# An attention and MLP kernel: the first batch's pieces in another hand-written order, two units' queries transposed twice, other engines for some copies

## The chip, the cores and the metric

The kernel runs on one core of a Trainium2 chip (trn2). The metric is the device time of one execution in microseconds (us); the kernel before was executed three times without the profiler, and once more with it. Engines are named as in the profile: PE (TensorE matmuls) and PEld (its weight loads), DVE (VectorE), ACT (ScalarE), POOL (GpSimd), SP (SyncE, which here only issues transfers). Each engine works through its own queue in order and waits on semaphores for what the others produce.

## The reference

For each of 8 batches and 12 heads, attention with normalised queries and keys, over 448 tokens and 64 columns a head; then, for each token, a normalisation over the 768 joined columns and a two-layer MLP that is added to its input.

```
def rmsnorm(x, g):
    rms = np.sqrt(np.mean(x * x, axis=-1, keepdims=True) + 1e-06)
    return x / rms * g
q_n, k_n = (rmsnorm(q, g_q), rmsnorm(k, g_k))
scores = np.matmul(q_n, k_n.transpose(0, 1, 3, 2)) / np.sqrt(64)
attn = softmax(scores)                      # written out in the original
x = np.matmul(attn, v)                      # heads joined: (8, 448, 768)
xn = (x - mean(x)) / np.sqrt(var(x) + 1e-06) * g_ln
out = x + np.maximum(xn @ w_ch1, 0.0) @ w_ch2   # 768 -> 3072 -> 768
```

## The kernel before

**Units, pairs, groups.** Two heads make a pair; a batch has 6 pairs. Pairs are prepared in units: batch 0 has units 0 and 1 of one pair each (pairs 0 and 1), units 2 and 3 of two pairs each (2 and 3, 4 and 5); every later unit has two pairs. A pair's 448 tokens form 7 groups of 128 rows: six of 128 tokens of one head, and one with the last 64 tokens of both heads.

**Preparing a unit.** `pieces` gives each step a letter, which the order below uses: b begin, a and c the squares of keys and queries (`square`), d and e their sums (`total`), g, gk, gq the reciprocal roots (`root`: two short ACT instructions), i the keys times the product of the two gains (`kg`), j the keys' high part in 16 bits (`khi`), k their low part (`klo`), l the scaled queries (`qn`), m a second copy of the queries beside the first (`qdup`), z the values. Constants at the head of the file say which engine does a step for which unit: `DVE_KG`, `POOL_HI`, `POOL_DUP`, `POOL_SQUARE`, `POOL_LO`, and `ACT_Q`, `ACT_K`, `ACT_DUP` for copies that otherwise go to DVE or POOL. The keys' high and low parts stand side by side as 128 columns, so that one product with the doubled queries adds both.

**Transposes.** K*p* (`trans_k`) transposes pair p's seven key groups by small matmuls with an identity into the PSUM tile "tr" and copies them to `kU`; Q*p* (`trans_q`) does the same with the queries, for pairs of batch 0 by way of a PSUM tile "psQ" of its own, for pair 6 and later by "tr". Units listed in `TWICE` skip the copy m: `trans_q` transposes the 64 query columns twice, into partitions 0 to 63 and into 64 to 127, by two half-width matmuls a group.

**Attention.** S*p.i* (`scores`) multiplies one group's keys with all queries into one of two PSUM banks "psS", and ACT takes the exponential (line 433), which frees the bank. The seventh group of the first units takes two accumulating matmuls (lines 427, 428). V*p.i* (`values`) multiplies the exponentials with the values (lines 470, 472); after i = 6, DVE divides (lines 485 to 492). T*p* gathers statistics on DVE.

**The order.** For batch 0 the whole work is written out by hand in `ORDER`: `first_attention` goes through it and records each piece on its engine, and this is the order of every engine's queue. It holds seven pairs' scores (pair 6 is batch 1's first). H*n* stands for n matmuls of the identity with itself on a PSUM tile "psW" that nothing reads (line 544), J*n* for n such on "tr" (line 547). L*u* loads unit u by SP, W*c* loads weights by POOL's queue, A, N, X, R are the first MLP's normalisation and its transposes (line 710), U*t* the first products of the MLP (line 956). After it, `run_rest` runs batch b's MLP on PE (first lines 730 and 740, later 809 and 832) with the next batch's attention spread between its matmuls.

Of the kernel before, what the change touches and what calls it, by code (L numbers as in the profile page):

```python
# [34 lines left out]


ORDER = """
b0 H12 a0 L4 c0 i0 e0 j0 H24 b1 gq0 d0 k0 l0 a1 m0 K0 G gk0 i1 H10 L5 c1 Q0 d1 j1 H8 S0.0 b2  # L40
S0.1 H5 a2 e1 g1 S0.2 c2 S0.3 k1 l1 z0 d2 e2 m1 K1 S0.4 i2 H16 S0.5 S0.6 H12 Q1 g2 H5 J8 b3 l2
j2 k2 c3 V0.0 S1.0 z2 S1.1 S1.2 V1.0 J8 a3 m2 H4 V0.1 z3 S1.3 K2 S1.4 V0.2 Q2 V0.3 V0.4 d3 S1.5
V0.5 V0.6 S2.0 S1.6 V1.1 V1.2 S2.1 e3 W0 i3 K3 V2.0 S2.2 V2.1 S2.3 Q3 j3 T0 S2.4 k3 V1.3 g3 V1.4
S2.5 S2.6 l3 b4 V1.5 m3 c4 S3.0 S3.1 V2.2 S3.2 K4 a4 V1.6 S3.3 V2.3 S3.4 Q4 d4 V2.4 V2.5 V3.0
V3.1 V3.2 V2.6 i4 S3.5 j4 J4 S3.6 V3.3 T1 K5 e4 k4 S4.0 W1 S4.1 S4.2 Q5 z4 b5 S4.3 V3.4 V4.0
V3.5 S4.4 V4.1 V4.2 S4.5 W2 V4.3 S5.0 g4 V3.6 S4.6 S5.1 J4 V5.0 V4.4 G2 S5.2 l4 T3 K6 V4.5 V5.1
V4.6 S5.3 T4 V5.2 a5 L6 V5.3 S5.4 m4 Q6 i5 S5.5 V5.4 S5.6 V5.5 V5.6 T5 S6.0 S6.1 J4 S6.2 A V6.0
S6.3 V6.1 N0 N1 S6.4 S6.5 J4 V6.2 X0 V6.3 d5 j5 N2 S6.6 V6.4 X1 z5 Q7 c5 V6.5 R U0 e5 U1 g5 X2
V6.6 M k5 U2 K7 b6 L7 a6 L8k c6 i6 l5 m5 e6
""".split()  # L50
# [44 lines left out]
class _Fast:  # L95
# [141 lines left out]
    def pieces(self, u):  # L237
# [91 lines left out]
        def qdup():  # L329
            if u in TWICE:  # L330
                return
            out, x = c["qn"][:, :, 1], c["qn"][:, :, 0]
            if u in ACT_DUP:
                nc.scalar.copy(out=out, in_=x)
            else:
                (nc.gpsimd if u in POOL_DUP else nc.vector).tensor_copy(out=out, in_=x)
# [50 lines left out]
    def trans_q(self, p):  # L387
# [6 lines left out]
        for i in (6, *range(6)):  # L394
            o, g = ps[:, :, 384:S] if i == 6 else ps[:, i // 3, ts(i % 3, 128)], self.group(p, i)
            for r in (slice(0, D), slice(D, 2 * D)) if u in TWICE else (slice(0, 2 * D),):
                nc.tensor.matmul(o[r], qn[:, g, 0] if u in TWICE else qn[:, g], sh.id16,
                                 is_transpose=True, start=(i == 6), stop=(i == 5))
# [866 lines left out]
```

## Time and profile before

| What | us |
| --- | --- |
| median of 3 runs | 578.69 |
| lowest and highest | 578.44, 578.82 |
| the profiled execution | 578.23 |
| its span, first to last instruction | 576.70 |
| PE busy in the span | 563.6 (98%) |
| PEld | 416.5 (72%) |
| DVE | 385.5 (67%) |
| ACT | 363.4 (63%) |
| POOL | 210.0 (36%) |

The rows shown further on come from the profiled execution; times in them count from the start of its span. A row of the timeline has start, length, engine, line, operation, output<-inputs, how many instructions it merges, and in brackets how long the engine was idle before it and what ended that. Matmuls are pipelined, so the length of one is more than the distance to the next; the same holds, by about 0.1 us, for neighbouring ACT and DVE instructions. A row of the stretches has the length of the stretch, each engine's busy time and instructions, the TensorE clock's granted share, the DMA engines' share and GB/s.

### The profile page before, as it was taken

How to read it: one execution, taken by the hardware profiler on the slowest of the kernel's cores; microseconds unless marked ns; L12 is line 12 of the kernel's file. 1: busy time of each engine (PE TensorE's matmuls, PEld its weight loads, DVE VectorE, ACT ScalarE, POOL GpSimd, SP SyncE). 2: the span in 40 equal slices, each digit the busy share in tenths (PEclk: the TensorE clock that was granted, in tenths of full speed). 3: DMA queues.
4: the chain of work that ended last, by engine and by line, in shares of the span. 5: the costliest groups of instructions: out<-in, count | busy, mean ns of one | idle time of the engine just before them, and what ended most of it. 6: DMA issues, size and time to landing. Idle time of an engine off the chain costs nothing.

```text
span 576.7 us, 13800 instructions
## 1 busy us (share of the span) xinstructions
PE 563.6 (98%) x5510; PEld 416.5 (72%) x5510; DVE 385.5 (67%) x832; ACT 363.4 (63%) x672; POOL 210.0 (36%) x226
## 2 busy tenths in 40 slices
PE   6888999999999999999999999999999999999999
PEld 5656666687686867777677768777777777878686
DVE  6989578799757586846667586854756743664424
ACT  5998886457674779457675588647777477323130
POOL 4885855404540721554341521654242410020000
PEclk9999999999999999999999999999999999999999
DMA  8999999968573877968563787958753390030302
GB/s 215 272 237 221 212 200 165 170 180 111 124 134 84 145 151 141 127 140 116 124 91 66 183 139 143 117 139 141 129 62 65 120 112 2 1 109 1 84 2 59
DMA packets 175321, 72.59 MB, mean 126 GB/s; under 512 B 138292, under 2 KB 170212, under 8 KB 175252
## 3 DMA queue, kind: packets, MB, share of 16 engines
q1 hardware_dynamic: 134304, 52.75, 43.9%
q0 software_dynamic: 40352, 18.50, 24.1%
q8 instruction: 44, 0.72, 0.5%
q10 hardware_dynamic: 596, 0.41, 0.3%
q14 instruction: 25, 0.20, 0.1%
HBM read 52.76 MB, written 11.01 MB: 111 GB/s over the span
## 4 chain that ended last, share of the span: by engine, by line
PE 92%; DVE 3%; ACT 3%; issue 1%; DMA 0%; ACTq 0%; DVEq 0%
PE psH L809 34%; PE psP L832 30%; PE psS L417 8%; PE oA L470 5%; PE psC L740 4%; PE psH L730 4%; ACT E L433 2%; PE oB L472 2%; PE psS L423 2%; DVE ssq L269 1%; PE psW L544 1%; PE tr L380 1%; ACT qU L400 0%; PE psW L1003 0%; DMA w<-in_g_k_dram 0%
## 5 line engine op out<-in xcount | busy, mean ns | idle before, releaser
L433 ACT ACTIVATE E<-psS,rr_all 128x448 f16<-128x448 f32 x336 | 204.1, 633 | 49.1 <-PE psS L417 40.4
L809 PE MATMUL psH<-xnT,w 128*128 128x256 f16 (+1 forms) x2016 | 225.7, 261 | 0.0
L809 PEld LDWEIGHTS <-w 128*128 128x128 f16 x2016 | 172.8, 98 | 24.4 <-issue 5.0
L812 ACT ACTIVATE hS<-psH 128x512 f16<-128x512 f32 x150 | 89.7, 598 | 98.0 <-PE psH L809 93.3
L832 PEld LDWEIGHTS <-hS 128*128 128x128 f16 x1080 | 100.0, 98 | 57.4 <-issue 1.1
L832 PE MATMUL psP<-w,hS 128*128 128x384 f16 x672 | 127.0, 326 | 0.0
L417 PE MATMUL psS<-qU,kU 128*128 128x448 f16 x288 | 101.0, 352 | 4.4 <-ACT E L433 2.9
L470 PEld LDWEIGHTS <-E 128*128 128x128 f16 x1008 | 70.3, 98 | 35.6 <-issue 2.6
L283 POOL TENSOR_TENSOR k<-k,gprod 128x896 f32<-128x896 f32 x18 | 39.2, 2180 | 139.8 <-ACT khl L263 86.1
L815 DVE TENSOR_TENSOR hS<-hS 128x512 f16<-128x512 f16 (+1 forms) x119 | 58.3, 496 | 19.3 <-ACT hS L812 17.8
L832 PE MATMUL psP<-w2s,hS 128*128 128x384 f16 (+1 forms) x408 | 69.9, 322 | 0.0
L470 PE MATMUL oA<-v,E 128*128 128x65 f16 x864 | 66.8, 194 | 1.1 <-ACT E L433 0.6
L768 DVE SCALAR_TENSOR_TENSOR x<-psP,rs_all,x 128x384 f32<-128x384 f32 x60 | 36.4, 616 | 41.1 <-PE psP L832 40.5
L472 PE MATMUL oB<-v,E 128*128 128x65 f16 x288 | 52.0, 193 | 0.1
L843 POOL TENSOR_TENSOR x<-x,hS 128x384 f32<-128x384 f32 x21 | 23.4, 1126 | 75.3 <-ACT hS L911 74.6
L485 DVE RECIPROCAL rec_all<-oA 128x6 f32<-128x6 f32 x48 | 9.2, 192 | 53.0 <-PE oA L470 52.9
L220 POOL DMA_DIRECT2D v<-in_v_dram x54 | 41.5, 781 | 4.4 <-PE oB L472 3.3
L417 PEld LDWEIGHTS <-kU 128*128 128x128 f16 x288 | 28.1, 98 | 10.7 <-issue 2.0
L911 ACT ACTIVATE hS<-hS,rs_all 128x384 f32<-128x384 f32 x27 | 14.6, 604 | 33.0 <-DVE hS L815 33.0
L472 PEld LDWEIGHTS <-E 128*128 128x128 f16 x336 | 32.4, 97 | 0.3 <-DVE xl L492 0.2
L86 DVE SCALAR_TENSOR_TENSOR qn<-q,rr_all 128x256 f16<-128x256 f32 (+2 forms) x69 | 25.0, 424 | 6.8 <-ACT rr_all L273 6.7
L269 DVE TENSOR_REDUCE ssq<-khl 128x14 f32<-128x896 f32 (+1 forms) x24 | 25.5, 1061 | 3.7 <-ACT khl L263 3.6
(145 smaller groups left out, 630.5 us busy)
## 6 DMA issues: line engine op xcount, KB each, us to landing
k<-in_k_dram SPq DMA_DIRECT2D x19, 384.0 KB, 4.3
q<-in_q_dram SPq DMA_DIRECT2D x18, 384.0 KB, 4.1
out_dram<-x SPq DMA_DIRECT2D x14, 384.0 KB, 3.0
w<-in_moe_w_ch_dram POOLq DMA_DIRECT2D x3, 1536.0 KB, 14.5
w<-in_moe_w_ch_dram POOLq DMA_DIRECT2D x4, 1152.0 KB, 14.1
v<-in_v_dram POOLq DMA_DIRECT2D x54, 64.0 KB, 4.4
out_dram<-x POOLq DMA_DIRECT2D x9, 384.0 KB, 2.7
qU<-qn SPq DMA_TRANSPOSE x90, 2.9
```

Source lines behind the costliest of these rows:

```text
L220: nc.gpsimd.dma_start(out[:, :, j, 0:D], main[:, :, j])
L269: nc.vector.tensor_reduce(out=c["ssq"][:, n], in_=c["sq", n], axis=AX.X, op=ALU.add)
L283: (nc.vector if u in DVE_KG else nc.gpsimd).tensor_tensor(out=c["t"][1], in0=c["t"][1], in1=sh.gprod.unsqueeze(1).broadcast_to([128, g, D] ...
L417: nc.tensor.matmul(ps[0][:, 0:S], c["main"][:, ts(i, 128)], c["q"][:, ts(h, S)], start=True, stop=True)
L433: nc.scalar.activation(out=o, in_=x[:, 0:S], func=AFT.Exp, scale=self.units[u][3][:, g:g + 1], bias=EXP_BIAS)
L470: nc.tensor.matmul(oA[:, t, cs], E[:, ts(t, 128)], rhs, start=(i == 0 and t == 0), stop=(i == 6 and t == 2))
L472: nc.tensor.matmul(oB[:, cs], E[:, 320:448], rhs, start=(i == 0), stop=(i == 6))
L768: self.nc.vector.scalar_tensor_tensor(out=x, in0=ps, scalar=self.rs[:, b, t:t + 1], in1=x, op0=ALU.mult, op1=ALU.add)
L809: nc.tensor.matmul(ps[:, i], sh.w1[:, dc, ts(f + i, 128)], self.xnT[:, dc, 256 - N:256], start=(i == 0 and dc == 0), stop=(i == k - 1 and ...
L812: nc.scalar.activation(out=hT[:, f:f + k], in_=ps, func=AFT.Relu)
L815: nc.vector.tensor_tensor(out=out, in0=a, in1=c, op=op)
L832: nc.tensor.matmul(bank[x][:, c], a[:, f], w[:, f, c], start=(start and f == 0), stop=(stop and f == HALF - 1))
```

## The change

`ORDER` is rewritten; it holds the same 218 pieces of work. Its identity matmuls on "psW" go from 96 to 144, those on "tr" from 32 to 4. Units 0 and 2 skip the second copy of their queries: the 21 query transposes of pairs 0, 2 and 3 become 42 of half width. Together PE gets 41 matmuls more. Homes that change: unit 1's and unit 2's key multiply from POOL to DVE, unit 6's from DVE to POOL; unit 1's high part from POOL to ACT; unit 1's second query copy from DVE to ACT; pair 0's key copy out of PSUM from DVE to ACT; pair 0's and pair 2's query copy from ACT to DVE; the square of unit 6's queries from POOL to ACT. SP's queue stays as it was.

```
-DVE_KG, POOL_HI, POOL_DUP, ACT_Q = (0, 6), (1, 2, 3, 4, 5, 6, *range(8, 25)), (3, 4, 5, 6), (0, 2, 4, 5)
-ACT_K, ACT_DUP = (), ()
+DVE_KG, POOL_HI, POOL_DUP, ACT_Q = (0, 1, 2), (2, 3, 4, 5, 6, *range(8, 25)), (1, 3, 4, 5, 6), (4, 5)
+ACT_K, ACT_DUP = (0,), (0, 1, 2)
 END_WORK = 44
-TWICE = ()
-POOL_SQUARE, POOL_LO = ((2, 1), (4, 0), (6, 0), (7, 0), (7, 1)), (5, 6)
+TWICE = (0, 2)
+POOL_SQUARE, POOL_LO = ((2, 1), (4, 0), (7, 0), (7, 1)), (5, 6)

 ORDER = """
-b0 H12 a0 L4 c0 i0 e0 j0 H24 b1 gq0 d0 k0 l0 a1 m0 K0 G gk0 i1 H10 L5 c1 Q0 d1 j1 H8 S0.0 b2
-S0.1 H5 a2 e1 g1 S0.2 c2 S0.3 k1 l1 z0 d2 e2 m1 K1 S0.4 i2 H16 S0.5 S0.6 H12 Q1 g2 H5 J8 b3 l2
-j2 k2 c3 V0.0 S1.0 z2 S1.1 S1.2 V1.0 J8 a3 m2 H4 V0.1 z3 S1.3 K2 S1.4 V0.2 Q2 V0.3 V0.4 d3 S1.5
-V0.5 V0.6 S2.0 S1.6 V1.1 V1.2 S2.1 e3 W0 i3 K3 V2.0 S2.2 V2.1 S2.3 Q3 j3 T0 S2.4 k3 V1.3 g3 V1.4
...
-V3.5 S4.4 V4.1 V4.2 S4.5 W2 V4.3 S5.0 g4 V3.6 S4.6 S5.1 J4 V5.0 V4.4 G2 S5.2 l4 T3 K6 V4.5 V5.1
-V4.6 S5.3 T4 V5.2 a5 L6 V5.3 S5.4 m4 Q6 i5 S5.5 V5.4 S5.6 V5.5 V5.6 T5 S6.0 S6.1 J4 S6.2 A V6.0
-S6.3 V6.1 N0 N1 S6.4 S6.5 J4 V6.2 X0 V6.3 d5 j5 N2 S6.6 V6.4 X1 z5 Q7 c5 V6.5 R U0 e5 U1 g5 X2
-V6.6 M k5 U2 K7 b6 L7 a6 L8k c6 i6 l5 m5 e6
+b0 H26 L4 b1 a0 c0 i0 e0 j0 gq0 G a1 k0 H10 l0 d0 H9 c1 i1 gk0 L5 d1 m0 K0 H8 Q0 e1 j1 b2 k1 H13
+S0.0 a2 S0.1 H26 H10 g1 i2 c2 S0.2 S0.3 H4 l1 m1 d2 H8 z0 j2 S0.4 V0.0 H2 e2 H5 S0.5 g2 Q1 K1 b3
+z2 c3 H8 z3 V0.1 H7 V0.2 S1.0 l2 S0.6 V0.3 k2 m2 S1.1 a3 H8 d3 V0.4 S1.2 V0.5 V1.0 S1.3 V1.1 K2
+S1.4 Q2 S1.5 S1.6 V0.6 S2.0 S2.1 e3 T0 S2.2 V1.2 V2.0 g3 V2.1 S2.3 i3 j3 k3 W0 K3 S2.4 V2.2 Q3
...
+V3.6 S4.5 W2 V4.0 V4.1 V4.2 g4 V4.3 S4.6 G2 S5.0 K6 T3 V4.4 S5.1 l4 V5.0 S5.2 S5.3 V5.1 V5.2
+S5.4 m4 V4.5 L6 V4.6 S5.5 T4 S5.6 b5 V5.3 a5 Q6 V5.4 V5.5 V5.6 S6.0 i5 T5 S6.1 J4 S6.2 S6.3 S6.4
+V6.0 S6.5 A N0 N1 V6.1 X0 V6.2 S6.6 X1 N2 Q7 V6.3 U0 d5 j5 R X2 V6.4 V6.5 U1 L7 L8k c5 M K7 e5
+U2 z5 b6 V6.6 a6 k5 g5 l5 m5 c6 i6 e6
 """.split()
```

More of the change, by code (lines that the diff above doesn't have):

```diff
@@ L27 @@
 EXP_BIAS = -4.0
-DVE_KG, POOL_HI, POOL_DUP, ACT_Q = (0, 6), (1, 2, 3, 4, 5, 6, *range(8, 25)), (3, 4, 5, 6), (0, 2, 4, 5)
-ACT_K, ACT_DUP = (), ()
+DVE_KG, POOL_HI, POOL_DUP, ACT_Q = (0, 1, 2), (2, 3, 4, 5, 6, *range(8, 25)), (1, 3, 4, 5, 6), (4, 5)
+ACT_K, ACT_DUP = (0,), (0, 1, 2)
 END_WORK = 44
-TWICE = ()
-POOL_SQUARE, POOL_LO = ((2, 1), (4, 0), (6, 0), (7, 0), (7, 1)), (5, 6)
+TWICE = (0, 2)
+POOL_SQUARE, POOL_LO = ((2, 1), (4, 0), (7, 0), (7, 1)), (5, 6)
 ORDER = """
-b0 H12 a0 L4 c0 i0 e0 j0 H24 b1 gq0 d0 k0 l0 a1 m0 K0 G gk0 i1 H10 L5 c1 Q0 d1 j1 H8 S0.0 b2
-S0.1 H5 a2 e1 g1 S0.2 c2 S0.3 k1 l1 z0 d2 e2 m1 K1 S0.4 i2 H16 S0.5 S0.6 H12 Q1 g2 H5 J8 b3 l2
-j2 k2 c3 V0.0 S1.0 z2 S1.1 S1.2 V1.0 J8 a3 m2 H4 V0.1 z3 S1.3 K2 S1.4 V0.2 Q2 V0.3 V0.4 d3 S1.5
-V0.5 V0.6 S2.0 S1.6 V1.1 V1.2 S2.1 e3 W0 i3 K3 V2.0 S2.2 V2.1 S2.3 Q3 j3 T0 S2.4 k3 V1.3 g3 V1.4
-S2.5 S2.6 l3 b4 V1.5 m3 c4 S3.0 S3.1 V2.2 S3.2 K4 a4 V1.6 S3.3 V2.3 S3.4 Q4 d4 V2.4 V2.5 V3.0
-V3.1 V3.2 V2.6 i4 S3.5 j4 J4 S3.6 V3.3 T1 K5 e4 k4 S4.0 W1 S4.1 S4.2 Q5 z4 b5 S4.3 V3.4 V4.0
-V3.5 S4.4 V4.1 V4.2 S4.5 W2 V4.3 S5.0 g4 V3.6 S4.6 S5.1 J4 V5.0 V4.4 G2 S5.2 l4 T3 K6 V4.5 V5.1
-V4.6 S5.3 T4 V5.2 a5 L6 V5.3 S5.4 m4 Q6 i5 S5.5 V5.4 S5.6 V5.5 V5.6 T5 S6.0 S6.1 J4 S6.2 A V6.0
-S6.3 V6.1 N0 N1 S6.4 S6.5 J4 V6.2 X0 V6.3 d5 j5 N2 S6.6 V6.4 X1 z5 Q7 c5 V6.5 R U0 e5 U1 g5 X2
-V6.6 M k5 U2 K7 b6 L7 a6 L8k c6 i6 l5 m5 e6
+b0 H26 L4 b1 a0 c0 i0 e0 j0 gq0 G a1 k0 H10 l0 d0 H9 c1 i1 gk0 L5 d1 m0 K0 H8 Q0 e1 j1 b2 k1 H13
+S0.0 a2 S0.1 H26 H10 g1 i2 c2 S0.2 S0.3 H4 l1 m1 d2 H8 z0 j2 S0.4 V0.0 H2 e2 H5 S0.5 g2 Q1 K1 b3
+z2 c3 H8 z3 V0.1 H7 V0.2 S1.0 l2 S0.6 V0.3 k2 m2 S1.1 a3 H8 d3 V0.4 S1.2 V0.5 V1.0 S1.3 V1.1 K2
+S1.4 Q2 S1.5 S1.6 V0.6 S2.0 S2.1 e3 T0 S2.2 V1.2 V2.0 g3 V2.1 S2.3 i3 j3 k3 W0 K3 S2.4 V2.2 Q3
+S2.5 V1.3 b4 S2.6 V1.4 S3.0 a4 S3.1 V2.3 c4 V1.5 S3.2 l3 V1.6 V2.4 V2.5 d4 T1 S3.3 m3 S3.4 Q4
+V3.0 K4 i4 S3.5 j4 e4 S3.6 Q5 W1 V3.1 V2.6 V3.2 V3.3 S4.0 K5 V3.4 S4.1 V3.5 S4.2 z4 S4.3 S4.4 k4
+V3.6 S4.5 W2 V4.0 V4.1 V4.2 g4 V4.3 S4.6 G2 S5.0 K6 T3 V4.4 S5.1 l4 V5.0 S5.2 S5.3 V5.1 V5.2
+S5.4 m4 V4.5 L6 V4.6 S5.5 T4 S5.6 b5 V5.3 a5 Q6 V5.4 V5.5 V5.6 S6.0 i5 T5 S6.1 J4 S6.2 S6.3 S6.4
+V6.0 S6.5 A N0 N1 V6.1 X0 V6.2 S6.6 X1 N2 Q7 V6.3 U0 d5 j5 R X2 V6.4 V6.5 U1 L7 L8k c5 M K7 e5
+U2 z5 b6 V6.6 a6 k5 g5 l5 m5 c6 i6 e6
 """.split()
```

## The prediction

> **What bounds the kernel now.** I read the page first, then a table of stretches, then each engine's timeline from 0 to 57 us, where all of the change lies. The table gives each stretch's length and each engine's busy us, with instruction counts:
>
> ```profile
> core 0: us, PE busy (x) PEld busy (x) DVE busy (x) ACT busy (x) POOL busy (x), PEclk, DMA share, GB/s
> 0.00:12.90 12.90, 8.11 (x72) 7.22 (x73) 8.00 (x21) 5.84 (x12) 5.29 (x12) 1.00 0.83 205
> 12.90:51.20 38.30, 31.62 (x411) 21.84 (x410) 35.45 (x68) 35.52 (x67) 28.15 (x27) 1.00 1.09 250
> ...
> 56.40:576.70 520.30, 519.07 (x4948) 382.78 (x4945) 336.94 (x735) 318.34 (x586) 172.40 (x184) 1.00 0.65 114
> ```
>
> From 56.4 us on TensorE is busy 519.07 of 520.30 us, so nothing but TensorE work sets that stage, and a shift of its start passes to the end one for one. Before that, three stages: a start in which one chain runs from the first load to the first exponential; 38 us in which ScalarE holds 35.5 us of work; and a tail of transposes and first products. The 49 exponentials of the middle (42 of the first six pairs, 7 of the seventh):
>
> ```profile
> L433 ACT ACTIVATE E<-psS,rr_all 128x448 f16<-128x448 f32 x49 | 28.4, 631 | 2.3 <-PE psS L417 1.8
> L400 ACT COPY qU<-psQ 128x896 f16<-128x896 f16 x3 | 2.7, 908 | 0.0
> ```
>
> **The start, step by step.** These are the rows up to the first exponential (start, length):
>
> ```profile
> 2.73 1.46 PE L544 MATMUL psW<-id 128*128 128x128 f16 x12 [2.73 <-POOL id masks.py:199]
> 5.70 0.69 PE L281 MATMUL psG<-gprod,w 1*128 1x64 f32 x2 [1.51 <-DVE gprod L278]
> 6.32 2.74 PE L544 MATMUL psW<-id 128*128 128x128 f16 x24
> 9.09 0.85 PE L380 MATMUL tr<-id,khl 128*128 128x128 f16 x6
> 9.73 1.27 PE L544 MATMUL psW<-id 128*128 128x128 f16 x10
> 10.80 0.74 PE L397 MATMUL psQ<-id,qn 128*128 128x128 f16 x7
> 11.37 0.61 PE L544 MATMUL psW<-id 128*128 128x128 f16 x8
> 12.53 0.54 PE L417 MATMUL psS<-qU,kU 128*128 128x448 f16 x2 [0.55 <-ACT qU L400]
> ...
> 7.81 0.61 DVE L269 TENSOR_REDUCE ssq<-w2s 128x7 f32<-128x448 f32 x1
> 8.34 0.62 DVE L294 TENSOR_TENSOR khl<-w2s,khl 128x448 f16<-128x448 f32 x1
> 8.87 0.62 DVE L86 SCALAR_TENSOR_TENSOR qn<-w2s,rr_all 128x448 f16<-128x448 f32 x1
> 9.52 1.11 DVE L336 COPY qn<-qn 128x448 f16<-128x448 f16 x1
> ...
> 8.93 1.55 POOL L283 TENSOR_TENSOR w2s<-w2s,gprod 128x448 f32<-128x448 f32 x1 [4.92 <-ACT khl L263]
> ...
> 7.40 0.58 ACT L291 ACTIVATE khl<-w2s 128x448 f16<-128x448 f32 x1 [1.26 <-DVE w2s L283]
> 11.57 0.91 ACT L400 COPY qU<-psQ 128x896 f16<-128x896 f16 x1 [1.81 <-PE psQ L397]
> 12.91 1.16 ACT L433 ACTIVATE E<-psS,rr_all 128x448 f16<-128x448 f32 x2 [0.44 <-PE psS L417]
> ```
>
> Queries of unit 0 are normalised until 9.49, copied beside themselves until 10.63 (1.11 us, drawn out by the POOL multiply, which ends at 10.48), transposed from 10.80, copied out by ScalarE until 12.48, and the first exponential begins at 12.91. TensorE's clock is seen in the spacing of equal small matmuls: 24 in 2.74 us stand (2.74 - 0.31) / 23 = 106 ns apart, 10 from 9.73 still 106 ns, 8 from 11.37 (0.61 - 0.22) / 7 = 56 ns. So full speed comes at about 11.2 us, inside the seven query transposes, 5.5 us after TensorE became steadily busy at 5.70.
>
> In the changed queues the copy L336 of unit 0 is gone, and one reduction (L269, step 8.34 - 7.81 = 0.53 us) moves behind the low-part subtraction L294. That then waits only for ScalarE's cast, until 7.40 + 0.58 = 8.0, and the normalisation L86 ends near 8.0 + 0.53 + 0.62 = 9.2 instead of 9.49. TensorE: 26 fillers to about 5.5, psG, 19 fillers from 6.32 to 8.35, the key transposes from about 8.7, 8 fillers, then the queries. At the slow clock this puts the queries at 8.7 + 7 x 0.107 + 8 x 0.107 = 10.3, at the fast one at 8.7 + 15 x 0.056 = 9.5.
>
> The query transposes are now 14 of half width, which write partitions 0 to 63 and 64 to 127 in turn. No transpose like that is in the trace; the nearest rows are the leftover scores of later units, 64 weight columns each and the two halves alternating:
>
> ```profile
> L423 PEld LDWEIGHTS <-kU x80: 106/108/110, 73.9 to 482.8; 128*64 128x64 f16 x80
> ...
> 73.90 0.59 PE L423 MATMUL psS<-qU,kU 128*64 128x448 f16 x4
> ...
> 74.42 1.15 PE L730 MATMUL psH<-w2s,w 128*128 128x384 f16 x6
> ```
>
> Four of them take 0.59 us with a median length of 0.37, so the first and the last start 0.22 us apart: two pairs, each pair side by side (one after the other it would be 3 x 0.187 = 0.56). A pair of 448 columns takes 0.21 where 448 columns alone take 0.187, so 23 ns are added for each pair; and the next full-width matmul stands 0.52 - 0.21 - 0.19 = 0.12 us late. I take 0.1 us at each end of a group and 23 ns a pair: 14 cost 0.2 + 7 x 0.078 = 0.75 us fast and 0.2 + 7 x 0.13 = 1.1 us slow. Bounds: 7 x 0.056 = 0.4 us (pairs for nothing), and 14 x 0.108 = 1.5 us (each behind its own 108 ns weight load). For the 42 half-width transposes of pairs 0, 2 and 3 the upper bound is 2.2 us above my price. The lower one is 1.1 us below it.
>
> VectorE, not ScalarE, now copies these queries out (0.62 us, by the L402 row below), but two reductions and unit 1's key multiply stand before it until about 10.7. So at the fast clock the copy ends near 11.3; at the slow clock the transposes end at 11.5 and the copy at 12.1. ScalarE meanwhile copies the keys, 128x960 out of PSUM, which no row shows: 0.91 x 960 / 896 = 0.97 by the L400 row (not under the 0.62 of VectorE, not over 1.3, twice an exponential of half the size), and casts unit 1's keys (0.58, as the first cast L291 of this shape), which holds it to about 11.6. The first score and 0.4 us later the first exponential: 11.8 to 12.5 instead of 12.91. **Start: -0.4 us if the clock is released when it was, -1.1 us if before 9.5 us.**
>
> **The clock.** TensorE will be busy from 2.73 with one hole of 0.2 us (5.5 to 5.7) where it stood idle from 4.19 to 5.70. Counting 5.5 us of steady work as in the row above puts the release at 8.2; if it hangs on the moment and not on the work, at 11.2. The Trainium skill, TensorE: Matmul & The Clock Gate, Part 1, says that a busy window of about 3.4 us that runs freely releases the clock; by that rule it would come between 6.1 and 9.6, and the trace's 5.5 us neither confirms nor excludes it.
>
> **The middle.** ScalarE waits that show:
>
> ```profile
> 17.60 0.91 DVE L336 COPY qn<-qn 128x448 f16<-128x448 f16 x1
> 18.56 0.56 PE L397 MATMUL psQ<-id,qn 128*128 128x128 f16 x7 [0.47 <-DVE qn L336]
> 19.16 0.95 ACT L263 ACTIVATE qn<-w2s 128x896 f32<-128x896 f32 x1 [0.70 <-PE psQ L397]
> ...
> 41.20 1.09 DVE L86 SCALAR_TENSOR_TENSOR qn<-hS,rr_all 128x896 f16<-128x896 f32 x1
> ...
> 43.31 0.66 DVE L385 COPY kU<-tr 128x960 f16<-128x960 f16 x1
> ...
> 45.92 0.62 DVE L402 COPY qU<-tr 128x896 f16<-128x896 f16 x1
> ...
> 42.70 0.63 ACT L433 ACTIVATE E<-psS,rr_all 128x448 f16<-128x448 f32 x1 [0.41 <-PE psS L417]
> 47.04 3.30 ACT L433 ACTIVATE E<-psS,rr_all 128x448 f16<-128x448 f32 x6 [0.95 <-PE psS L417]
> 51.17 0.65 ACT L433 ACTIVATE E<-psS,rr_all 128x448 f16<-128x448 f32 x1
> ```
>
> (a) 0.70 us: the square of unit 3's queries may not overwrite the buffer before unit 1's queries are transposed, and these wait for VectorE's copy at 17.60. That copy goes to ScalarE (0.58), ahead of TensorE's need. (b) 0.41 and 0.95 us: pairs 5 and 6 wait for keys and queries whose copies L385 and L402 stand on VectorE behind L86 and the statistics; the new order sets the seventh pair's key copy ahead of both, and TensorE's transposes then free the shared bank "tr" in time. That is 2.06 us of waits. Walking the new queues with the lengths of the old rows I find smaller ones in their place: 0.3 to 0.4 us each where unit 2's root waits for the totals of VectorE (which now also multiplies unit 2's keys), and twice where the two-part leftover score and a run of half-width transposes stand between two scores; 0.8 us together. So idle -1.3. Work: one query copy fewer in the stretch (3 to 2; 0.91 less 0.1 overlap, as exponentials of 0.63 follow each other at 0.53), one duplication more (0.58 - 0.1): -0.3. **Middle: -1.6 us.** The same walk with the old queues gives 12.99 and 51.13 for the first and the 49th exponential, which the trace has at 12.91 and 51.17; inside the stretch it strays by up to 0.4 us, so each wait is good to no more than that.
>
> The 48 more fillers on psW and 28 fewer on the bank "tr", 56 ns each: 20 x 0.056 = 1.1 us of TensorE, beside its idle time (31.62 busy of 38.30), so they cost nothing while they only fill; the 36 between the second and third score (2.0 us) stand beside two exponentials (0.53 each), a square (0.95 - 0.1) and a root's two short instructions on ScalarE, 1.9 us and a little more. Without that cover, each is 56 ns on the chain.
>
> **The tail.** The last exponential to the MLP's own matmuls:
>
> ```profile
> 55.04 1.17 PE L956 MATMUL psU<-w2s,w 128*128 128x128 f16 x18 [0.42 <-DVE w2s L718]
> 56.44 2.60 PE L730 MATMUL psH<-w2s,w 128*128 128x384 f16 x15
> ```
>
> 56.44 - 51.17 = 5.27 us. The third token tile is normalised ahead of the squares' total, and its transposes go before the second group of psU, so the 0.42 us wait for its copy goes: **-0.4 us**. Unit 6's multiply leaves VectorE for POOL and its query square leaves POOL for ScalarE (0.94), both after 55 us where ScalarE has 318 us of work in 520; uncovered, they would delay the next pairs' scores by about 1 us. SP issues the same transfers in the same order; POOL's first weight load moves behind one multiply and cast, and is read first by the psU matmuls of the tail. The tightest transfer later on:
>
> ```profile
> 86.23 1.70 POOL L628 DMA_DIRECT2D w<-in_moe_w_ch_dram x2
> ...
> DMA to landing us min/median/max: 11.1/14.1/19.2
> ...
> 106.69 0.99 PE L740 MATMUL psC<-w,hS 128*128 128x384 f16 x5
> ```
>
> Its second half lands at worst at 87.1 + 19.2 = 106.3, by the median at 101.2, and is read at 106.69. With TensorE 2.7 us earlier the read comes at 104.0; the issue follows a key transpose that moves along. So no new wait at the median.
>
> **Sum.** -0.4 - 1.6 - 0.4 = -2.4 us with the clock as before, -3.1 with it early; no row decides, I take -2.7. The profiled execution took 578.23 us (span 576.70, 1.53 around it) and would take 575.5; the runs' median of 578.69 stands 0.46 above it, so **576.0 us**.
>
> **Rivals.** (1) Half-width transposes one after another: +2.2 of PE time, of which about 2 falls between scores: -2.7 + 2.0, 578.0. For: weight loads of 106 ns; against: the 0.59 us row. (2) New waits take the place of the old: unit 1's normalisation stands behind the multiply that VectorE takes over, and if this meets POOL as L336 did at 9.52, the 1.3 us of idle stays: 577.3. (3) Slower: the clock is released late, because 21 transposes lie between 8.7 and 11.5. Decided at the 36 fillers; if they are still 107 ns apart, the 99 fillers and some 35 transposes up to 21 us cost 134 x 0.051 = 6.8 us more, of which TensorE's idle time absorbs 2.4:
>
> ```profile
> 12.00:24.00 12.00, 9.64 (x131) 7.18 (x131) 11.44 (x13) 10.59 (x21) 11.61 (x14) 1.00 1.05 278
> ```
>
> 12.00 - 9.64 = 2.4, so 576.0 + 4.4 = 580.4. For: before, the clock rose within the queries' transposes, and there were fewer of them. Against: 11 transposes (7 of keys, 4 of queries) stood ahead of 11.2 and did not prevent it. The skill's same page, Part 4, says that transposes do not count as busy; by it this rival gains, the row speaks against it. (4) It does not do what it says: the waits that go hid others as long just behind them; the 49th exponential stays and the time with it, 578.7. For: both late waits sit where all engines are busy; against: walking the queues shows none so long.
>
> **How the numbers follow.** Forecast 0.70 (575.0 to 576.8); (1) 0.10, (2) 0.10, (3) 0.07, (4) 0.03. The low end is -3.1 with free pairs, -3.7: 575.0; the high end takes in (2) and half of (1): 577.9. Beyond 0.2% (1.16 us, about what this measurement can tell) lie the forecast, most of (2) and a third of (1): faster 0.79, same 0.13, slower 0.08.
>
> **What would show it.** Right: first exponential at 11.8 to 12.5, the 49th 36.6 us later, no wait over 0.5 us there, pairs of half-width transposes 78 ns apart, MLP matmuls from 53.4 to 54.1, and from there the same 520 us. Wrong: fillers still 107 ns apart after 12 us; L397 groups of 1.5 us; waits of 0.7 us or more on psS; or TensorE idle for over 2 us after 56 us.

## The result and the profile after

| What | before | after |
| --- | --- | --- |
| median of 22 runs each, side by side, us | 578.40 | 581.00 |
| lowest and highest | 577.72, 579.95 | 578.17, 584.43 |
| the profiled execution | 578.23 | 581.10 |
| its span | 576.70 | 579.60 |
| its first exponential of pair 0 | 12.91 | 11.83 |
| its 49th exponential | 51.17 | 49.54 |
| its first own matmul of the MLP (L730) | 56.44 | 54.47 |

The ratio is 1.0037 (95% interval 1.0024 to 1.0050): the change is slower by some 2 us (the medians differ by 2.6) where a gain to 576.0 us was forecast. The runs after are spread over 6 us, those before over 2. The table splits the loss: up to the first L730 the changed kernel gains 1.97 us; from there to the end of the span it takes 579.60 - 54.47 = 525.13 us instead of 576.70 - 56.44 = 520.26, so 4.87 us are lost behind that point.

The stretches after, with the columns of those before:

```profile
57.02:60.43 3.41, 0.73 (x5) 0.29 (x3) 1.09 (x1) 1.72 (x4) 1.21 (x2) 1.00 0.98 258
60.43:63.84 3.41, 2.77 (x10) 1.28 (x10) 2.08 (x2) 2.79 (x7) 3.41 (x3) 0.50 0.66 160
```

TensorE is idle for 3.41 - 0.73 + 3.41 - 2.77 = 3.32 us, and the clock column falls to 0.50 for one stretch, where 2.77 us of work at half speed lose 1.39. Together that is 4.71 of the 4.87 us. The timeline of TensorE after:

```profile
2.74 2.95 PE L544 MATMUL psW<-id 128*128 128x128 f16 x26 [2.74 <-POOL id masks.py:199]
...
6.07 1.23 PE L544 MATMUL psW<-id 128*128 128x128 f16 x19
...
9.38 0.58 PE L397 MATMUL psQ<-id,qn 128*64 128x128 f16 x14
...
43.48 0.56 PE L397 MATMUL tr<-id,qn 128*128 128x128 f16 x7 [0.86 <-POOL qn L336]
...
45.05 0.54 PE L417 MATMUL psS<-qU,kU 128*128 128x448 f16 x2 [0.54 <-DVE qU L402]
...
54.47 2.60 PE L730 MATMUL psH<-w2s,w 128*128 128x384 f16 x15
...
57.09 0.65 PE L730 MATMUL psH<-w2s,w 128*128 128x384 f16 x3
61.07 1.12 PE L730 MATMUL psH<-w2s,w 128*128 128x384 f16 x3 [3.32 <-ACT hS L733]
```

The first 26 fillers stand (2.95 - 0.31) / 25 = 106 ns apart, the 19 from 6.07 on (1.23 - 0.22) / 18 = 56 ns: the clock is released by 6.07 us instead of 11.2. The last row is the loss: a matmul into an "mlp" bank waits until ScalarE has evicted an earlier one. ScalarE's timeline says why it had not:

```profile
11.83 1.16 ACT L433 ACTIVATE E<-psS,rr_all 128x448 f16<-128x448 f32 x2
...
17.68 0.95 ACT L263 ACTIVATE qn<-w2s 128x896 f32<-128x896 f32 x1 [0.47 <-DMA w2s<-in_q_dram]
...
45.50 3.31 ACT L433 ACTIVATE E<-psS,rr_all 128x448 f16<-128x448 f32 x6 [1.49 <-PE psS L417]
...
49.54 0.65 ACT L433 ACTIVATE E<-psS,rr_all 128x448 f16<-128x448 f32 x1
...
56.70 0.95 ACT L263 ACTIVATE khl<-k 128x896 f32<-128x896 f32 x1 [1.62 <-DMA k<-in_k_dram]
...
59.69 0.95 ACT L263 ACTIVATE qn<-q 128x896 f32<-128x896 f32 x1 [1.66 <-DMA q<-in_q_dram]
60.55 0.85 ACT L733 ACTIVATE hS<-psH 128x384 f16<-128x384 f32 x2
```

Ahead of the evictions L733 stand the squares of unit 6's keys and queries, and each waits for its load. Those loads, in the view of the tile "q" (the issue with its start, and the times from issue to landing of its three parts), before and after:

```profile
L149 SPq DMA_DIRECT2D q<-in_q_dram x1: 594/594/594, 35.3 to 35.3; - x1
...
DMA to landing us min/median/max: 6.4/6.5/7.7
```

```profile
L149 SPq DMA_DIRECT2D q<-in_q_dram x1: 1539/1539/1539, 39.2 to 39.2; - x1
...
DMA to landing us min/median/max: 13.0/18.6/19.9
```

Issued 3.9 us later, the load takes three times as long. What else was put in flight shows on POOL's timeline; L619 are the second and third load of the first MLP weight, 1536 KB each. Before and after:

```profile
36.27 0.89 POOL L619 DMA_DIRECT2D w<-in_moe_w_ch_dram  x1
...
38.52 0.82 POOL L619 DMA_DIRECT2D w<-in_moe_w_ch_dram  x1
```

```profile
33.52 0.89 POOL L619 DMA_DIRECT2D w<-in_moe_w_ch_dram  x1
...
35.78 0.82 POOL L619 DMA_DIRECT2D w<-in_moe_w_ch_dram  x1
```

Before, the first part of unit 6's queries was issued 1.0 us ahead of the second weight load; after, it comes 5.7 us behind it and 3.4 behind the third. The view of L619 after has the third load's landing:

```profile
L619 POOL DMA_DIRECT2D w<-in_moe_w_ch_dram x1: 821/821/821, 35.8 to 35.8; - x1
...
DMA to landing us min/median/max: 22.8/22.8/22.8
```

It lands at 35.8 + 22.8 = 58.6, and the queries at 39.2 + 19.9 = 59.1, as if they came after it. From this came theory T: a load that SP issues behind weight loads lands about when these are through, and an engine that works in order stands on it ahead of something that TensorE needs.

### The profile page after: what moved, and what is told of

Its sections match the earlier page's. It is cut to its first block, busy times and chain, and to the rows that moved or that the text cites. A ratio compares the mean times of both kernels' runs of the same rounds, so it can differ in the third digit from the quotient of the medians.

```text
span 579.6 us, 13875 instructions
## 1 busy us (share of the span) xinstructions
PE 564.3 (97%) x5551; PEld 416.4 (72%) x5551; DVE 382.4 (66%) x831; ACT 364.3 (63%) x674; POOL 203.4 (35%) x223
## 4 chain that ended last, share of the span: by engine, by line
PE 89%; SPq 5%; DMA 5%; issue 0%; ACT 0%; ACTq 0%
PE psH L809 34%; PE psP L832 30%; PE psS L417 8%; PE oA L470 5%; PE psC L740 4%; SPq L157 3%; PE psH L730 3%; DMA q<-in_q_dram 2%; PE psS L423 2%; PE oB L472 2%; SPq L149 1%; DMA k<-in_k_dram 1%; DMA w<-in_v_dram 1%; DMA w2s<-in_q_dram 1%; PE psW L1003 0%; PE tr L397 0%
## 5 line engine op out<-in xcount | busy, mean ns | idle before, releaser
L283 POOL TENSOR_TENSOR k<-k,gprod 128x896 f32<-128x896 f32 x19 | 41.4, 2177 | 141.5 <-ACT khl L263 116.1
L815 DVE TENSOR_TENSOR hS<-hS 128x512 f16<-128x512 f16 (+1 forms) x119 | 58.3, 496 | 19.3 <-ACT hS L812 17.8
L86 DVE SCALAR_TENSOR_TENSOR qn<-q,rr_all 128x256 f16<-128x256 f32 (+2 forms) x69 | 25.3, 428 | 6.9 <-ACT rr_all L273 6.8
L269 DVE TENSOR_REDUCE ssq<-khl 128x14 f32<-128x896 f32 (+1 forms) x24 | 25.5, 1062 | 5.4 <-ACT khl L263 5.1
```

The costliest lines, as they stand in the source:

```text
L269: nc.vector.tensor_reduce(out=c["ssq"][:, n], in_=c["sq", n], axis=AX.X, op=ALU.add)
L283: (nc.vector if u in DVE_KG else nc.gpsimd).tensor_tensor(out=c["t"][1], in0=c["t"][1], in1=sh.gprod.unsqueeze(1).broadcast_to([128, g, D] ...
L815: nc.vector.tensor_tensor(out=out, in0=a, in1=c, op=op)
```

## The experiments

Fifteen kernels were run. Where nothing else is said they start from the kernel after. The edits show only the part of a line that changes, with -/+ as in a diff. A name like e6_unit6_weights_late, in short e6, is a run; the pieces of `ORDER` have letters and numbers too, and are called pieces. "Queries" gives, from each profile, when the first part of unit 6's queries was issued and when it landed (issue plus time to landing).

| run | median, us | lowest, highest | ratio to before (95%) | 2nd weight load issued | queries |
| --- | --- | --- | --- | --- | --- |
| before | 578.4 | 577.7, 580.0 | | 36.27 | 35.3, 41.7 |
| after | 581.00 | 578.2, 584.4 | 1.0037 (1.0024 to 1.0050) | 33.52 | 39.2, 59.1 |
| e1_weights_late | 576.54 | 576.0, 582.9 | 0.9983 (0.9963 to 1.0004) | 37.64 | 37.0, 43.3 |
| e2_square_pool | 581.51 | 578.1, 582.8 | 1.0041 (1.0028 to 1.0054) | 34.23 | 35.3, 59.2 |
| e3_both | 577.70 | 577.3, 578.8 | 0.9986 (0.9978 to 0.9995) | 36.88 | 36.8, 44.2 |
| e4_before_both | 579.87 | 578.7, 580.8 | 1.0019 (1.0010 to 1.0028) | 33.40 | 42.1, 59.2 |
| e5_unit6_late | 577.82 | 576.9, 578.3 | 0.9981 (0.9967 to 0.9995) | 33.57 | 34.6, 59.4 |
| e6_unit6_weights_late | 576.71 | 575.7, 581.0 | 0.9974 (0.9956 to 0.9993) | 37.40 | 34.2, 52.0 |
| e7_12_fillers | 577.47 | 575.8, 584.6 | 0.9995 (0.9969 to 1.0021) | 37.34 | 35.7, 44.0 |
| e8_full_width | 577.61 | 576.9, 579.1 | 0.9984 (0.9970 to 0.9998) | 38.00 | 35.3, 45.5 |
| e9_l4_first | 576.68 | 575.9, 577.3 | 0.9966 (0.9954 to 0.9979) | 37.66 | 33.8, 47.4 |
| e10_w2_later | 577.47 | 575.4, 581.4 | 0.9986 (0.9969 to 1.0004) | 36.89 | 35.3, 47.3 |
| e11_60_fillers | 581.62 | 580.5, 582.4 | 1.0048 (1.0035 to 1.0060) | 33.78 | 42.5, 60.4 |
| e12_before_weights | 579.55 | 578.8, 581.8 | 1.0020 (1.0009 to 1.0031) | 33.20 | 41.8, 58.0 |
| e13_t4_later | 576.48 | 575.5, 578.3 | 0.9971 (0.9962 to 0.9980) | 37.80 | 36.5, 46.4 |
| e14_w0_later | 579.81 | 578.3, 582.4 | 1.0031 (1.0016 to 1.0047) | 37.83 | 30.6, 36.3 |
| e15_before_square | 578.24 | 577.5, 579.6 | 1.0000 (0.9991 to 1.0009) | 36.15 | 39.5, 56.3 |

### The weights later

```
-S3.6 Q5 W1 V3.1
+S3.6 Q5 V3.1
...
-S4.5 W2 V4.0
+S4.5 V4.0
...
-S4.6 G2 S5.0
+S4.6 G2 W1 W2 S5.0
```

> The changed kernel, with the second and third load of the first MLP weight (L619) issued behind POOL's scaling of gln, at about 37 and 38 us instead of 33.5 and 35.8 (36.3 and 38.5 before the change). Theory T, the weights stand ahead: 3 MB of weights, issued before the last part of unit 6's keys (37.6 us) and before its queries (39.2 to 46.6 us), hold these up in the DMA engines; ScalarE then stands in its queue on the square of unit 6's queries ahead of the MLP's evictions. With the weights later the queries land by about 50 us instead of 59.6, the wait of 3.32 us on L733 goes, TensorE's clock does not fall, and the time is 576 us (0.996 of the kernel before). Rival R, the slip: SP's queue was already 1.0 us late at 12 us and 2.2 us late at 28 us, and that alone makes unit 6 land late; then the queries still land after 55 us, the wait stays over 2 us, and the time stays at 580 to 581.

The view of the tile "q", and then TensorE's timeline at the place of the loss:

```profile
L149 SPq DMA_DIRECT2D q<-in_q_dram x1: 595/595/595, 37.0 to 37.0; - x1
...
DMA to landing us min/median/max: 6.3/6.3/6.3
```

```profile
54.51 2.60 PE L730 MATMUL psH<-w2s,w 128*128 128x384 f16 x15
...
57.13 1.14 PE L730 MATMUL psH<-w2s,w 128*128 128x384 f16 x6
```

Two places moved on one engine's queue take 4.5 us off the median, and the 2 us gained ahead of the MLP now reach the end: 576.54 against 578.53 for the runs of before beside it. SP issued unit 6's keys no earlier than in the changed kernel (30.5 us against 30.2), so the slip of SP's queue, rival R, was not the cause. Eight of the 12 runs lie between 576.0 and 576.7 and four between 578.1 and 582.9, so the interval still touches 1.

A weight load need not stand ahead to hold up a load. The first part of unit 6's keys is issued ahead of the second weight load both times, at 30.2 us after and at 30.5 in e1; it lands after 23.2 us in the one (53.4) and after 11.5 in the other (42.0). The profile's counts for the two DMA queues show why:

| stretch, us | run | POOL's queue: packets, MB | SP's queue: packets, MB |
| --- | --- | --- | --- |
| 28 to 34 | e14 | none | 2445, 1.36 |
| 40 to 46 | after | 506, 1.04 | 509, 0.27 |
| 36.3 to 39.5 | before | 40, 0.06 | 1530, 0.87 |
| 36.3 to 39.5 | after | 262, 0.51 | 343, 0.22 |
| 38 to 41 | e1 | 31, 0.04 | 1545, 0.87 |
| 38 to 41 | e6 | 92, 0.17 | 1234, 0.72 |

While weights move, both queues get about as many packets through, and the weights' packets are four times as large (2.1 KB against 0.5), so SP's queue moves a fifth of the bytes. Before the change, and in e1, there is a pause of some 3 us between the first and the second weight load, in which SP's queue moves 0.87 MB and unit 6's loads get through. In the changed kernel the second weight load is issued while the first still moves, and the pause is gone.

### The square on POOL, alone and with the weights later

```
-POOL_SQUARE, POOL_LO = ((2, 1), (4, 0), (7, 0), (7, 1)), (5, 6)
+POOL_SQUARE, POOL_LO = ((2, 1), (4, 0), (6, 0), (7, 0), (7, 1)), (5, 6)
```

> The changed kernel, with the square of unit 6's queries back on POOL; the transfers are as in the changed kernel. T: the queries still land at about 59 us, but nothing that TensorE needs stands behind them; ScalarE waits only for unit 6's keys (57.7 us with the square), the wait on L733 shrinks from 3.3 to about 1 us, the clock stays up: 577 us. R2, ScalarE's queue is not what holds TensorE (the wait belongs to the keys or to the transfers as such): the wait stays at about 3 us and the time at 580 to 581.

> Both edits of the two runs before: the weights later and the square on POOL. T: nothing is left of the loss; MLP matmuls from about 54.4 us without a wait over 0.5 us, 576.0 us or a little under (0.996). R or any loss that sits elsewhere (in the 520 us behind the first matmuls of the MLP): over 577.5.

In e2 TensorE no longer waits for L733; another wait takes its place. VectorE's and TensorE's timelines of e2:

```profile
62.77 1.08 DVE L269 TENSOR_REDUCE ssq<-qn 128x14 f32<-128x896 f32 x1 [4.62 <-POOL qn L261]
63.77 1.08 DVE L269 TENSOR_REDUCE ssq<-khl 128x14 f32<-128x896 f32 x1
64.88 0.66 DVE L385 COPY kU<-tr 128x960 f16<-128x960 f16 x1
```

```profile
65.59 0.55 PE L397 MATMUL tr<-id,qn 128*128 128x128 f16 x7 [3.55 <-DVE kU L385]
```

The square has left ScalarE, but its sum (the piece e6, L269) stands in VectorE's queue ahead of the key copy that frees "tr", and so TensorE waits 3.55 us there. My expectation of 577 us was wrong by this: I had looked at ScalarE's queue alone. In e3 the queries land in time, yet the same wait is 1.60 us, because POOL reaches the square late; the 577.70 of e3 against 576.54 of e1 is that.

### The same two edits in the old order

```
-V3.2 V2.6 i4 S3.5 j4 J4
+V3.2 V2.6 W1 i4 S3.5 W2 j4 J4
...
-k4 S4.0 W1 S4.1
+k4 S4.0 S4.1
...
-S4.5 W2 V4.3
+S4.5 V4.3
```

These three start from the kernel before. e12 has this edit alone, e15 alone the square of unit 6's queries on ScalarE, and e4 has both.

> The kernel before, with the two things that T blames put in: second and third weight load ahead of POOL's multiply and cast of unit 4's keys (about 33 and 36 us instead of 36.3 and 38.5), and the square of unit 6's queries on ScalarE. T: the queries land at 50 us or later instead of 45.3, ScalarE stands on their square behind 57 us, TensorE waits 1 to 3 us on L733, and the time is 579 to 582. R: SP's queue has no slip here, so unit 6 lands as before and the time is within 0.5 us of the kernel before.

> The kernel before with the two weight loads alone moved ahead of POOL's work on unit 4's keys; the square of unit 6's queries stays on POOL. T: unit 6's queries land at 50 to 60 us as in e4_before_both; nobody on ScalarE stands on them, but VectorE's total of them stands ahead of a key copy that TensorE waits for, so a wait of up to 3 us shows on L397 behind L385 and the time is 579 to 581. If the square on ScalarE was the whole loss of e4_before_both: 578.5, the time of the kernel before.

> The kernel before with the square of unit 6's queries on ScalarE alone; the weights are loaded as before. With e12_before_weights (the weights alone, 579.55) and e4_before_both (579.87) this is the fourth corner. T: the queries land by about 45 us, the square costs ScalarE 0.95 us at a place where TensorE has bank to spare: 578.2 to 578.9. If the square ahead of the evictions costs by itself: 579.2 or more.

The weights alone (e12) cost 1.34 us against the runs of before beside them (579.55 - 578.21), the square alone (e15) 0.09, both (e4) 1.34. So the weights' place is the cause in the old order too. In e4's profile TensorE waits 1.21 us for L733. In e12 the wait is where it was expected, on VectorE's copy, though only 0.70 us of the 3 that were allowed:

```profile
63.99 0.55 PE L397 MATMUL tr<-id,qn 128*128 128x128 f16 x7 [0.70 <-DVE kU L385]
```

e15's profiled execution (579.62 us) was the slowest of its 11. SP's queue was late in it, the queries were issued at 39.5, behind the second weight load, and ScalarE stands on them:

```profile
59.60 0.95 ACT L263 ACTIVATE qn<-q 128x896 f32<-128x896 f32 x1 [1.97 <-DMA w2s<-in_k_dram]
```

(The row names another load; the third part of the queries, issued at 41.0, landed 18.5 us later, at 59.5.) TensorE waited 1.36 us for L733 in it. So the old order, too, passes this place by a narrow margin, and a run that loses the race pays for it.

### Unit 6's work later

```
-U2 z5 b6 V6.6 a6 k5 g5 l5 m5 c6 i6 e6
+U2 z5 b6 V6.6 k5 g5 l5 m5
...
-EARLY = {5: (42, 49), 6: (47, 56), 7: (61, 69), 8: (75, 83), 9: (89, 97)}
+EARLY = {5: (42, 49), 6: (51, 60), 7: (61, 69), 8: (75, 83), 9: (89, 97)}
```

`EARLY` gives, for each unit, between which steps of the MLP the rest of its preparation is spread. e6 has the later weight loads of e1 as well.

> The changed kernel with its weight loads where the change put them (33.5 and 35.8 us); moved are both squares of unit 6 and what hangs on them (its multiply, its totals, its root), from ahead of the MLP's first evictions to behind some of them. The transfers are as in the changed kernel. T (transfers late, and a queue in order that stands on them): unit 6's queries still land at 57 us or later, nothing that TensorE needs stands behind them, the waits on L733 and on L385 stay under 0.5 us, the clock stays up, and the time is 576 to 576.8 us. If late transfers cost time by themselves, whatever stands behind them, the wait turns up at another consumer and the time stays over 579.

> That edit together with the later weight loads of e1_weights_late. T: the same median as e1_weights_late or 0.3 us less, 576.0 to 576.6 us, and without its runs of 578 to 583 us, because a late landing now has no one to hold up.

In e5 the queries land as late as ever (59.4 us), TensorE does not wait for L733, and the median falls by 3.2 us: a late load costs what stands behind it. But 577.82 missed the 576 to 576.8 expected. TensorE's waits behind 48 us in e5:

```profile
PE psS L417 <- ACT E L433: 0.8, 1, 0.8
PE tr L397 <- DVE kU L385: 0.4, 1, 0.4
```

These 1.2 us are left, at 78.5 and 79.4 us: the delay reaches later consumers, POOL's square of unit 7's queries waits 2.18 us for its load until 74.6 us, and in e6 it does not wait. With the weights later as well (e6) TensorE waits nowhere behind 48 us, and the median is 576.71. It keeps a run of 578.0 and one of 581.0, against what was expected.

### The first weight load later, the third later still

```
-k3 W0 K3
+k3 K3
...
-i4 S3.5 j4 e4
+i4 S3.5 j4 W0 e4
```

and in e10

```
-G2 W1 W2 S5.0
+G2 W1 S5.0
...
-i5 T5
+i5 W2 T5
```

Both start from e6.

> e6_unit6_weights_late with the first weight load as well moved later, from about 26 to about 33.5 us. If a weight load in flight holds up every load that is issued behind it, the loads of units 5 and 6 (issued from 22 to 37 us) go free of it: unit 6's queries land within 10 us of their issue instead of 16 to 18, and the runs lie closer together, median 575.8 to 576.5. If the first weight load does not matter to them, landings and median stay; if it lands too late for the first MLP products (about 51 us), TensorE waits at psU and the time is over 577.

> e6_unit6_weights_late with the third weight load another 8 us later (at about 46 us, behind POOL's multiply of unit 5's keys). T: unit 6's and 7's loads meet one weight load less, the runs over 577.5 us go, the median is 576.0 to 576.6. If the third load then lands too late for the MLP's last matmuls of L730 (from about 72 us), TensorE waits there and the time is over 577.

e14 is the cleanest measurement of the cause: no weight load is in flight until 33.3 us, SP issues unit 6's queries at 30.6, and they land 5.7 us later. The view of the tile "q", and TensorE's waits behind 64 us:

```profile
L149 SPq DMA_DIRECT2D q<-in_q_dram x1: 594/594/594, 30.6 to 30.6; - x1
...
DMA to landing us min/median/max: 5.7/5.7/5.7
```

```profile
PE psC L740 <- DMA w<-in_moe_w_ch_dram: 2.5, 1, 2.5
```

As a remedy it fails: weights that start later end later, and L740 waits 2.5 us for the second MLP weight, the transfer that the prediction had called the tightest; the clock falls behind that wait (0.52 from 109.2 to 112.6 us). In e10 the third load at 45.9 us brought nothing (577.47, against 576.71 for e6, both widely spread).

### The clock behind the wait

```
+... [nc.tensor.matmul(self.tr[:, 192:320], sh.id16, sh.id16, is_transpose=True, start=True, stop=True) for _ in range(60 * (f == 6))]
```

> The changed kernel with 60 small transposes of the identity on TensorE (60 x 56 ns = 3.4 us) in front of the matmul that waits for L733. If the half clock from 60.4 to 63.8 us comes of the 3.3 us of idleness before it, the fillers keep the clock up, the wait itself stays, and the time falls by 1.2 to 1.7 us to about 579.5. If the clock fell for another reason, the time stays at 581 or rises.

The stretches of e11, its timeline of TensorE, and the row behind the MLP's last matmul in the timeline after:

```profile
57.02:60.43 3.41, 3.41 (x53) 3.06 (x52) 0.00 (x0) 0.85 (x1) 0.00 (x0) 1.00 0.74 197
60.43:63.84 3.41, 2.38 (x27) 1.68 (x25) 2.90 (x3) 3.28 (x9) 1.75 (x2) 1.00 0.77 217
```

```profile
57.84 3.51 PE L727 MATMUL tr<-id 128*128 128x128 f16 x60
62.38 0.65 PE L730 MATMUL psH<-w2s,w 128*128 128x384 f16 x3 [1.03 <-ACT hS L733]
...
575.72 2.62 PE L1003 MATMUL psW<-id 128*128 128x128 f16 x44
```

```profile
575.71 2.62 PE L1003 MATMUL psW<-id 128*128 128x128 f16 x44
```

The clock stays at 1.00, and three L730 matmuls take 0.65 us instead of 1.12: the half clock was a result of the idle time. The time did not fall: 581.62, where 579.5 was expected. In the profiled execution the loads landed 1.3 us later still, so the wait ended at 62.38 us instead of 61.07. From there to the fillers L1003 behind the MLP's last matmul it takes 575.72 - 62.38 = 513.34 us, against 575.71 - 61.07 = 514.64 after: 1.30 of the 1.39 us of the clock came back, and the later landing took them. The span is 1.2 us longer (580.8 against 579.6) by what follows these fillers' start, the storing of the results. Whether the fillers themselves make the loads land later is not shown.

### The start: fillers and half-width transposes

```
-b0 H26 L4
+b0 H12 L4
```

```
-TWICE = (0, 2)
+TWICE = ()
```

The first edit is e7, the second e8; both start from e1.

> e1_weights_late with 12 fillers instead of 26 at TensorE's start, as before the change, so that TensorE idles from about 4.2 to 5.6 us again. If the clock is released by a run of steady work, it comes up at 9 to 11.2 us instead of 5.8, the first exponential begins at 12.3 to 12.6 instead of 11.8, and the time is 0.5 to 0.8 us over e1_weights_late (577.1 to 577.3). If the clock hangs on something else (the moment, the first matmul), the clock comes up at 5.8 us and the time is unchanged within 0.2 us.

> e1_weights_late without the half-width transposes: units 0 and 2 are duplicated by ScalarE copies (0.58 and 0.91 us) and transposed at full width. By the prediction's price (14 half-width transposes 0.58 us in the trace after, 7 of full width 0.56 at full clock) the transposes themselves are even, and the copies stand on the chain: unit 0's first exponential 0.5 to 0.8 us later (12.3 to 12.6), unit 2's copy another 0.3 to 0.9 us of ScalarE, together 577.3 to 578.2 us. If the copies are hidden: 576.5.

TensorE's timeline of e7, then one row of that of e8:

```profile
2.74 1.46 PE L544 MATMUL psW<-id 128*128 128x128 f16 x12 [2.74 <-POOL id masks.py:199]
...
5.86 2.21 PE L544 MATMUL psW<-id 128*128 128x128 f16 x19
...
8.95 1.06 PE L544 MATMUL psW<-id 128*128 128x128 f16 x8
```

```profile
10.73 0.56 PE L397 MATMUL psQ<-id,qn 128*128 128x128 f16 x7 [0.99 <-ACT qn L334]
```

With the hole back (4.20 to 5.24 us), 19 fillers stand (2.21 - 0.31) / 18 = 106 ns apart and the 8 from 8.95 still 107: the clock is released after 10 us, so it hangs on TensorE's steady work, and the first exponential moves to 12.45. But the 49th comes at 49.29, no later than in e1 (49.58, from a first exponential at 11.54): what the start gains is waited away on the way, for e1's ScalarE waits 0.67 us for a score at 16.68 and 0.50 for the load of unit 3's queries at 18.19 (the row at 17.68 after), and e7's does not. The median, 577.47, is spread too widely to tell 0.9 us from nothing. e8 shows what the half-width transposes buy: ScalarE's copy stands on the chain, the first exponential comes at 12.46, the 49th at 50.11, and the median is 1.07 us over e1's. As e7 starts as late and has its 49th at 49.29, the gain lies less at unit 0 than behind it, where e8's ScalarE copies unit 2's queries as well (0.94 us).

### The seventh pair's wait

```
-K6 T3 V4.4 S5.1 l4
+K6 l4 T3 V4.4 S5.1
```

and in e13 also

```
-S5.5 T4 S5.6
+S5.5 S5.6
...
-a5 Q6 V5.4
+a5 Q6 T4 V5.4
```

Both start from e6.

> e6_unit6_weights_late with VectorE's normalisation of unit 4's queries (L86) ahead of the statistics (L653, 1.08 us) that stand before it. In the changed kernel the seventh pair's first exponential still waits 1.49 us, on a chain L86 41.35, POOL's copy L336 42.49, transposes 43.48, VectorE's copy L402 44.38, score 45.05. Theory M (that chain holds the middle): L86 starts 1 us earlier, the wait falls to 0.5 us or less, the 49th exponential comes 0.6 to 1.0 us earlier, and the time is 575.7 to 576.1 us. Rival: the statistics, 1 us later, hold up the tail (the aggregate and the normalisations behind it), and the first matmul of the MLP stays at 54.3 us: 576.5 us.

> e9_l4_first with the next statistics (L653, 0.68 us) also behind VectorE's copy of the seventh pair's queries (L402). In e9_l4_first the normalisation came 1 us earlier and yet the first score of that pair waited 1.0 us for L402, which now stood behind these statistics. M: with both out of the way the seventh pair's first exponential waits 0.5 us or less, the 49th exponential and the first matmul of the MLP come 0.5 to 0.9 us earlier, 575.8 to 576.2 us. Rival: VectorE is full up to the tail, the statistics taken out here come back in front of the aggregate, the first matmul of the MLP stays: 576.7.

VectorE's and TensorE's timelines of e9, then a row of ScalarE's of e13:

```profile
43.77 0.68 DVE L653 BATCH_NORM_STATS2 stat<-x 128x6 f32<-128x128 f32 x3
44.48 0.62 DVE L402 COPY qU<-tr 128x896 f16<-128x896 f16 x1
```

```profile
45.16 0.54 PE L417 MATMUL psS<-qU,kU 128*128 128x448 f16 x2 [1.01 <-DVE qU L402]
```

```profile
45.05 3.30 ACT L433 ACTIVATE E<-psS,rr_all 128x448 f16<-128x448 f32 x6 [0.38 <-PE psS L417]
```

In e9 the wait stays at 1.08 us on ScalarE (1.04 in e6): the normalisation is early, and the next statistics now stand before the copy. With these moved too (e13) it is 0.38 us, and yet the median is 576.48 against 576.68 and 576.71 (e9, e6). VectorE's normalisations for the MLP (L674) begin no earlier, at 47.51 us in e13 against 47.36 and 47.08, because the statistics return in front of them. So the rival holds as far as the medians can tell: VectorE's load in front of the tail takes the rest. e13's profiled execution (577.73 us) also shows the clock fall in the stage before the MLP; its stretches:

```profile
46.00:48.00 2.00, 1.37 (x12) 0.63 (x10) 1.94 (x9) 2.00 (x5) 0.82 (x1) 1.00 1.11 217
48.00:50.00 2.00, 1.67 (x13) 1.02 (x14) 2.00 (x4) 1.14 (x3) 0.00 (x0) 0.64 1.11 224
50.00:52.00 2.00, 2.00 (x23) 2.00 (x22) 0.84 (x2) 1.80 (x6) 0.00 (x0) 0.50 1.11 228
```

e9 and e13 have the lowest ratios: with the later weights and unit 6's work behind the first evictions they beat both kernels, by 0.3% against before. e1 and e6 are not told apart from them.

## Why the prediction was wrong

- **Start, -0.4 to -1.1 us: right, at its far end.** The first exponential came at 11.83, within 11.8 to 12.5, with the clock released by 6.07 us. The prediction left open whether work or the moment decides; e7 shows that it is steady work. The sum adds this gain to the middle's; e7, which starts 0.9 us later than e1 and has its 49th exponential no later, says that little of it gets past the middle.
- **Half-width transposes, 0.75 us for 14: over-priced.** They took 0.58 us, (0.58 - 0.22) / 13 = 28 ns apart, so a pair costs 56 ns and not 78: the lower bound, pairs for nothing. Rival (1) is out. e8 puts the worth of them, copies included, at 1.07 us.
- **Middle, -1.6 us: the right sign, a third of the size.** From the first to the 49th exponential it went from 38.26 to 37.71 us, -0.55. Of the three waits that were to go, the one at 42.70 went; the one at 19.16, the square of unit 3's queries, now waits for its load instead (0.47 at 17.68); and the one at 47.04 (0.95 us) came back as 1.49 at 45.50, behind the chain L86, L336, L397, L402 of the rows at 43.48 and 45.05. The prediction counted on the seventh pair's key copy standing ahead of L86; that pair's queries, which go through L86 and POOL's copy L336, had no such place, and the miss of about 1 us is more than the 0.4 us to which it trusted its walk. Rival (2), new waits for old, holds for the middle in its outcome, not in the mechanism it names: unit 1's normalisation took 0.61 us behind VectorE's multiply. The sign it gave, a wait of 0.7 us or more on psS, was seen.
- **Tail, -0.4 us: right.** 54.47 - 49.54 = 4.93 us against 5.27.
- **Sum up to the MLP: -1.97 us** against the -2.7 taken. Had "from there the same 520 us" held, the time would have been 576.7, inside the range, and e1 has it at 576.54.
- **The step that failed** is the sentence "SP issues the same transfers in the same order", with the conclusion "So no new wait at the median", drawn from one later transfer alone. SP's order is the same; it was never set against POOL's. The price list had POOL's first weight load, which moves behind a multiply and a cast, but not the second and third, which come 2.7 us earlier, because the square of unit 4's queries (1.67 us) no longer stands between the copy L336 and the multiply of unit 4's keys, and that copy starts 1.1 us earlier. So the pause between the first and the second weight load, which unit 6's loads had passed through, closed. The transfer that was tested for its landing, L628, was tested by its old latency. Unit 6's loads were not, and their latency is not a constant. In the table, queries issued behind the second weight load land between 56.3 and 60.4 us whatever their issue; those issued between the first and the second land between 41.7 and 47.4, in e6 at 52.0; with no weight load ahead (e14), 5.7 us after their issue. It cost 3.32 us of idle TensorE and 1.39 us of half clock, and ended the "same 520 us".
- **The second half of that step** was that unit 6's square on ScalarE would at worst "delay the next pairs' scores by about 1 us". An instruction that waits for a load costs its queue the wait, not its length, and the MLP's evictions stood behind it. e2 and e12 show that the engine hardly matters: on POOL, VectorE's sum takes over the part.
- **What would show it wrong** named the right sign, "TensorE idle for over 2 us after 56 us". No rival carried it: the slower case, the clock released late, was another mechanism, and did not occur.

What stays open: why single runs of e1, e6, e7 and e10 still reach 579 to 585 us, and why the seven runs of after that stay below 580.1 escape most of the loss; SP's issue times differ between the profiled executions by some us (28.0 to 33.9 us for unit 6's keys, with SP's queue the same), and a lost race with the weights, as in e15's profile, would do it, but these runs have no profile.

## What to carry to other kernels

Times from issue to landing belong to what else is in flight, ahead or just behind, so when a change moves a bulk load on one queue, set its issue against every load that the other queues issue in the same 10 us, not against its own queue alone. Then, for each load that may land late, list what stands behind its first reader on that engine, and behind the reader of that result: moving the reader to another engine moves the wait, while moving it behind the work that TensorE needs, or the bulk load behind the small ones, removes it. A walk through queues with fixed durations is good for the compute part (1.97 us found of 2.7), and blind for this.
